# Window attention, forward and backward: attention products as 64x64 tiles only, and early gradient turns moved

## The chip, the cores and the metric

The kernel runs on one core of a Trainium2 chip. The metric is the device time of one execution, in microseconds. Before the change, 17 runs gave a median of 1991.69 us (1986.32 to 2002.65). TensorE (PE) multiplies, VectorE (DVE) and ScalarE (ACT) do the elementwise work and empty PSUM, GpSimd (POOL) and SyncE (SP) issue DMAs.

## The reference

An image `x` of 256 x 256 pixels with 384 channels is cut into 1024 windows of 8 x 8 pixels (64 tokens). In each window, self-attention with one head:

```python
qkv = xw @ wqkv
q, k, v = qkv[..., :C], qkv[..., C:2 * C], qkv[..., 2 * C:]
p = softmax(einsum('bqc,bkc->bqk', q, k) * C ** (-0.5), axis=-1)
o = einsum('bqk,bkc->bqc', p, v) @ wo
```

The outputs are `o` and, for a given `grad_out`, the gradients of `x` (`out_1`), `wqkv` (`out_2`) and `wo` (`out_3`). All data are bf16.

## The kernel before

The weights are merged first: `A` holds wq times the transpose of wk (with the scale), `B` holds wv times wo, and `AT_sb`, `BT_sb` their transposes. Per window, with tokens `x` and output gradient `d`, the kernel then needs `y` (from `x` and `A`) and `z` (from `d` and `BT`) to form the scores and the gradient of the probabilities; `uq` = x B and `vq` = x AT as values; and the products of the probabilities `P` and of their score gradients `dS` with `uq`, `vq`, `z`, `y`, `x` and `d`. The output `o` is P times `uq`. The gradient of `x` (the sums named `pd`) is the transpose of P times `z`, plus the transpose of dS times `y`, plus dS times `vq`. `Uq` (dS times x, named `pu` in PSUM) and `Wq` (the transpose of P times d, `pw`) feed the weight gradients.

Work goes in 128 quads. A quad is 4 tiles `t` of 128 partitions, and a tile is two windows: window 0 in partitions 0 to 63 (`LO`), window 1 in 64 to 127 (`HI`). The program is a software pipeline over quads, written out by hand: `step(c, b, a, ahead)` (L330) works on three quads at once. Each engine executes its instructions in the order in which the code issues them. In a step stand, in this order: the scores of quad `b` (`scores`, L179, 24 small products into `sd`); its softmax and softmax gradient in six pieces (`soft`, L191, on DVE and ACT) between the eight projections that make `uq` and `vq` (`uv`, L230); the projection of `a`'s gradient to `z` (`project` kind 0); a DMA transpose of `ps`, which holds P and dS side by side (`turn`, L240, giving `PS`, that is P and dS turned); the loads of the quad three ahead; a piece of the weight gradient (`filler(1)`: twelve products `pg`, added on DVE to `GF_acc`, L317); attention of `c` for tiles 0 and 1 (`attend`, L250); the projection of `a`'s tokens to `y` (`project` kind 1); `to_tokens` (L174), a DMA transpose of `yz`, which gives `z` and `y` with tokens in partitions, `tok`; another filler; and attention of `c` for tiles 2 and 3.

TensorE can be used as one array of 128 x 128, as two column halves (128*64 in the profile), or as four tiles of 64 x 64, which work side by side. In `attend`, `both` (L258) issues four products of 64 x 64 (row half in, row half out: LO to LO, LO to HI, HI to LO, HI to HI). "Straight" products write the half that they read; "crossed" ones write the other half, and their two sums then lie in two PSUM banks, one called outer. `po` and `pd` were crossed, `pu` and `pw` straight. `token_part` (L265) multiplies `ps` with `tok`, contracting over all 128 partitions, P with `z` in one half and dS with `y` in the other, as 128*64 products. Around it, the switch `split[0]` (L149) makes the projection to `y` and the filler between the pairs issue each product as two column halves.

PSUM has eight banks in one pool (`ring`); each sum takes a bank, and its next use waits until the last one is copied out. The DMA transposes of `tok`, `PS`, and of the loaded gradient and tokens (`load_turn`, L129: `dT` and `xT` of the quad two ahead) and the loads of `x` all stand in SP's queue, in the order of the code. POOL's queue holds the loads of the gradient and the stores of both outputs (L296 to L301). For the first quads, TensorE does the turns instead (`turn_on_pe`, L137): the gradients of quads 1 to 3 are turned inside the softmax of the step that projects them (`grad_turn`, L144 and L349). Behind the last step, `weight_gradients` (L380) finishes.

Of the kernel before, what the change touches and what calls it, by code (L numbers as in the profile page):

```python
# [22 lines left out]
def kernel(  # L23
# [124 lines left out]
    ALL = False  # L148
    split = [ALL]  # L149

    def product(out, lhsT, rhs, start, stop):
        if split[0]:
            for h in (LO, HI):
                nc.tensor.matmul(out[h], lhsT=lhsT[:, h], rhs=rhs, start=start, stop=stop)  # L154
        else:
            nc.tensor.matmul(out, lhsT=lhsT, rhs=rhs, start=start, stop=stop)  # L156

    ENG = {"D": nc.vector.tensor_copy, "A": nc.scalar.copy}

    def project(st, kind, mo):  # L160
        if kind == 0 and mo == 0:
            st["yz"] = qp.tile([P, CK, QUAD, 4, WT], BF16, tag="yz", name="yz")
        yz = st["yz"]
        wgt, src = ((BT_sb, st["dT"]), (A_sb, st["xT"]))[kind]
        pj = ring.tile([P, QUAD, 2, WT], F32, tag="r")
        for m in range(CK):
            product(pj[:].rearrange("p t w k -> p (t w k)"), wgt[:, m, mo * P:(mo + 1) * P], src[:, :, m, :],
                    m == 0, m == CK - 1)
        if kind == 0:
            ENG[EV["z"][mo]](out=yz[:, mo, :, 0:4:3, :], in_=pj[:])  # L170
        else:
            ENG[EV["y"][mo]](out=yz[:, mo, :, 1:3, :], in_=pj[:])  # L172

    def to_tokens(st):  # L174
        st["tok"] = tok = qp.tile([P, CK, QUAD, 2, P], BF16, tag="tok", name="tok", bufs=3)
        nc.sync.dma_start_transpose(out=tok[:].rearrange("p m t b k -> p (m t b) k"),
                                    in_=st["yz"][:].rearrange("p m t s k -> p (m t s k)"))

    def scores(st):  # L179
        yz, xT = st["yz"], st["xT"]  # L180
# [10 lines left out]
    def soft(st, step):  # L191
# [25 lines left out]
        elif step == 4:  # L217
            st["pr"] = pr = sm.tile([P, QUAD, WT], F32, tag="pr", name="pr")
            for w, h in ((0, LO), (1, HI)):
                nc.vector.tensor_tensor(out=pr[h, :, :], in0=sd[h, :, w, :], in1=st["Pb"][h, :, :], op=ALU.mult)  # L220
            st["D"] = D = sm.tile([P, QUAD], F32, tag="D", name="D")
            nc.vector.tensor_reduce(out=D[:], in_=pr[:], axis=AX.X, op=ALU.add)
        else:
            pd = sm.tile([P, QUAD, WT], F32, tag="pd")
            nc.vector.tensor_tensor(out=pd[:], in0=st["Pb"][:], in1=over_k(st["D"][:]), op=ALU.mult)
            ps = st["ps"]
            for w, h, o in ((0, LO, HI), (1, HI, LO)):
                nc.vector.tensor_tensor(out=ps[o, :, w, :], in0=st["pr"][h, :, :], in1=pd[h, :, :], op=ALU.subtract)

    def uv(st, t, part):  # L230
        if t == 0 and part == 0:
# [10 lines left out]
        nc.sync.dma_start_transpose(out=dst[:].rearrange("p t s k -> p t (s k)"),  # L242
                                    in_=st["ps"][:].rearrange("p t w k -> p (t w k)"))

    def turned(st, n, t, h):
        if n in ("PT", "ST"):
            return st["PS"][h, t, int((n == "ST") == (h == LO)), :]
        return st[n][h, t, :]

    def attend(st, pair):  # L250
# [4 lines left out]
        def bank(name):  # L255
            return ring.tile([P, C], F32, tag="r", name=name)

        def both(straight, crossed, t, outer, **flags):  # L258
            for h, o, (dst, lhs, rhs), fl in ((LO, LO, straight, {}), (LO, HI, crossed, flags), (HI, LO, crossed, flags),
                                              (HI, HI, straight, {})):  # L260
                at = dst if dst is not crossed[0] else dst[outer if h == LO else 1 - outer]
                nc.tensor.matmul(at[o, :], lhsT=turned(st, lhs, t, h), rhs=st[rhs][h, t, :],  # L262
                                 **{"start": True, "stop": True, **fl})

        def token_part(t, pd, outer, **flags):  # L265
            for w, o in ((0, HI), (1, LO)):
                nc.tensor.matmul(pd[outer if w == 0 else 1 - outer][o, :], lhsT=st["ps"][:, t, w, :],  # L267
                                 rhs=st["tok"][:, :, t, w, :], **flags)

        def keep(name, dst, src):  # L270
            for outer in (0, 1):
                sb = ob.tile([P, C], BF16, tag=name, name=name)
                nc.scalar.copy(out=sb[:], in_=src[outer][:])  # L273
                stores.append((dst, sb, outer))

        t0, t1 = pair
        stores = []
        pu = [bank("pu")]
        po = [bank("po") for outer in (0, 1)]
        pd = [bank("pd") for outer in (0, 1)]  # L280
        token_part(t0, pd, 1, start=True, stop=False)
        both((pu[0], "ST", "xq"), (po, "PT", "uq"), t0, 1)
        (nc.vector.tensor_copy if t0 else nc.scalar.copy)(out=st["Uq"][:, t0, :], in_=pu[0][:])
        pw = [bank("pw")]
        both((pw[0], "Pb", "dq"), (pd, "ST", "vq"), t0, 1, start=False, stop=True)
        nc.vector.tensor_copy(out=st["Wq"][:, t0, :], in_=pw[0][:])
        pu.append(bank("pu"))
        both((pu[1], "ST", "xq"), (po, "PT", "uq"), t1, 0)
        keep("o", out_0, po)
        nc.vector.tensor_copy(out=st["Uq"][:, t1, :], in_=pu[1][:])  # L290
        pw.append(bank("pw"))
        both((pw[1], "Pb", "dq"), (pd, "ST", "vq"), t1, 0, start=True, stop=False)
        nc.vector.tensor_copy(out=st["Wq"][:, t1, :], in_=pw[1][:])
        token_part(t1, pd, 0, start=False, stop=True)
        keep("d", out_1, pd)
        for dst, sb, outer in stores:  # L296
            if outer:
                nc.gpsimd.dma_start(out=windows(dst, st, 2 * t1 + 1, 1), in_=sb[LO, :])
                nc.gpsimd.dma_start(out=windows(dst, st, 2 * t0, 1), in_=sb[HI, :])
            else:  # L300
                nc.gpsimd.dma_start(out=windows(dst, st, 2 * t0 + 1), in_=sb[:])  # L301

    fill = []

# [25 lines left out]
    def step(c, b, a, ahead):  # L330
# [24 lines left out]
        if b is not None and c is None:  # L355
            turn_blocks(woT_sb, wo_sb)
# [12 lines left out]
        C_(attend, (2, 3))  # L369

    G_ON_PE, X_ON_PE = 4, 1
# [45 lines left out]
    with tc.manual_schedule(engines=MANUAL):  # L417
# [31 lines left out]
        split[0] = False  # L449
        filler(1 << 30)  # L450
        weight_gradients(last)

# [29 lines left out]
```

## Time and profile before

| | |
|---|---|
| median of 17 runs | 1991.69 us |
| the profiled execution | 1994.89 us |
| its span, first to last instruction | 1993.1 us |
| instructions | 52529 |
| granted TensorE clock, mean | 0.999 |
| DMA moved | 423.66 MB, mean 213 GB/s |
| SP's queue (q1): packets, share of 16 engines | 935984, 80.9% |
| POOL's queue (q0): packets, share of 16 engines | 98304, 31.1% |

A row of the profile's timeline gives start, length (both in us), engine, line of the code, operation, tiles out<-in, tile shape of a matmul, shape of the data and count; rows that follow each other with the same form are merged. Matmuls are pipelined, so the length of one includes its way through the array; the distance between starts tells the pace. A row of the groups gives the total busy time, the mean of one in ns, and the idle time ahead of it with who ended it.

### The profile page before, as it was taken

Reading aid. Unit: us, or ns where it says so; the run is one execution under the profiler, and the core shown is the slowest. Engines: PE = TensorE matmul, PEld = TensorE weight load, DVE = VectorE, ACT = ScalarE, POOL = GpSimd, SP = SyncE. Lnnn points to the kernel's source line nnn. Section 1 sums busy time; section 2 is a strip of 40 time slices with the busy share of each in tenths; the row PEclk is TensorE's granted clock in tenths of the full one; section 3 lists DMA queues with packets and bytes.
Section 4 is the critical chain, followed back from the end, with each engine's and each line's share of the span. In section 5 each row is a group of like instructions: output and inputs, shape, how many; then the busy total and the mean of one; then the engine's idle time right before and its main releaser. Section 6 shows DMA issues by size and latency. Waiting matters only on the chain. (4 is left out here: it accounts for less than half of the span.)

```text
span 1993.1 us, 52529 instructions
## 1 busy us (share of the span) xinstructions
PE 1967.3 (99%) x19487; PEld 1123.5 (56%) x19487; DVE 1259.6 (63%) x2860; ACT 1461.7 (73%) x3357; POOL 1122.5 (56%) x2054
## 2 busy tenths in 40 slices
PE   8999999999999999999999999999999999999999
PEld 4555555555555555555555555555555555555555
DVE  4666666666666656666666666666666666666666
ACT  6877777777777777777777777777777777777774
POOL 2655555555556555555555565556555555555553
PEclk9999999999999999999999999999999999999999
DMA  7999999999999999999999999999999999999994
GB/s 168 215 218 215 203 226 213 218 207 229 213 217 225 213 207 222 220 215 212 215 222 215 222 210 220 216 222 224 219 219 216 210 221 207 217 223 213 219 210 107
DMA packets 1036032, 423.66 MB, mean 213 GB/s; under 512 B 918016, under 2 KB 1011200, under 8 KB 1035776
## 3 DMA queue, kind: packets, MB, share of 16 engines
q1 hardware_dynamic: 935984, 267.85, 80.9%
q0 software_dynamic: 98304, 151.39, 31.1%
q8 instruction: 152, 2.49, 0.5%
q10 hardware_dynamic: 1488, 1.08, 0.2%
q14 instruction: 104, 0.85, 0.2%
HBM read 101.84 MB, written 101.84 MB: 102 GB/s over the span
## 5 line engine op out<-in xcount | busy, mean ns | idle before, releaser
L301 POOL DMA_DIRECT2D out_dram<-o x256 | 139.1, 543 | 679.7 <-ACT o L273 666.1
L317 DVE TENSOR_TENSOR GF_acc<-pg,GF_acc 128x384 f32<-128x384 f32 x258 | 143.9, 558 | 526.1 <-PE pg L154 372.2
L273 ACT CAST o<-po 128x384 bf16<-128x384 f32 x512 | 221.7, 487 | 247.8 <-issue 247.6
L156 PEld LDWEIGHTS <-xT 128*128 128x128 bf16 x3072 | 291.7, 98 | 183.2 <-issue 1.5
L156 PE MATMUL pj<-AT_sb,xT 128*128 128x384 bf16 x1536 | 333.5, 326 | 0.8 <-DVE dT L91 0.8
L156 PE MATMUL pj<-B_sb,xT 128*128 128x384 bf16 x1536 | 333.5, 326 | 0.0
L127 POOL DMA_DIRECT2D dq<-in_grad_out_dram x512 | 273.9, 546 | 77.0 <-DMA out_dram<-o 35.6
L156 PE MATMUL pj<-dT,BT_sb 128*128 128x512 bf16 x1152 | 271.3, 381 | 14.4 <-DMA dT<-dq 6.6
L154 PE MATMUL pj<-xT,A_sb 128*64 128x512 bf16 x2304 | 270.2, 379 | 0.0
L238 ACT CAST uq<-pj 128x384 bf16<-128x384 f32 x512 | 247.5, 483 | 30.1 <-PE pj L156 26.0
L238 ACT CAST vq<-pj 128x384 bf16<-128x384 f32 x512 | 250.1, 488 | 2.4
L273 ACT CAST d<-pd 128x384 bf16<-128x384 f32 x512 | 227.4, 512 | 0.2 <-ACT o L273 0.2
L156 PEld LDWEIGHTS <-xq 128*128 128x128 bf16 x1572 | 153.5, 98 | 114.8 <-issue 0.3
L154 PEld LDWEIGHTS <-xq 128*64 128x64 bf16 x3000 | 166.5, 110 | 90.3
L216 ACT COPY ps<-Pb 64x256 bf16<-64x256 bf16 x256 | 103.2, 403 | 149.6 <-DVE Pb L213 148.1
L170 ACT CAST yz<-pj 128x512 bf16<-128x512 f32 x384 | 207.0, 642 | 3.2 <-PE pj L156 2.0
L172 ACT CAST yz<-pj 128x512 bf16<-128x512 f32 x384 | 208.4, 658 | 0.8 <-PE pj L154 0.6
L156 PEld LDWEIGHTS <-BT_sb 128*128 128x128 bf16 x1152 | 111.8, 98 | 141.4 <-DMA dT<-dq 14.7
L154 PEld LDWEIGHTS <-A_sb 128*64 128x64 bf16 x2304 | 130.8, 110 | 97.7 <-issue 0.4
L156 PE MATMUL pg<-Uq,xq 128*128 128x384 bf16 x1032 | 181.6, 326 | 0.0
L267 PE MATMUL pd<-tok,ps 128*64 128x384 bf16 x1024 | 177.5, 344 | 0.0
L262 PE MATMUL pu<-xq,PS 64*64 64x384 bf16 x1024 | 175.0, 335 | 2.4 <-DMA PS<-ps 2.2
(87 smaller groups left out, 3386.5 us busy)
## 6 DMA issues: line engine op xcount, KB each, us to landing
xq<-in_x_dram SPq DMA_DIRECT2D x512, 96.0 KB, 4.1
dq<-in_grad_out_dram POOLq DMA_DIRECT2D x512, 96.0 KB, 3.9
out_dram<-o POOLq DMA_DIRECT2D x256, 96.0 KB, 4.3
out_dram<-o POOLq DMA_DIRECT2D x512, 48.0 KB, 4.4
out_dram<-d POOLq DMA_DIRECT2D x256, 96.0 KB, 4.5
out_dram<-d POOLq DMA_DIRECT2D x512, 48.0 KB, 4.5
tok<-yz SPq DMA_TRANSPOSE x128, 8.3
PS<-ps SPq DMA_TRANSPOSE x128, 4.9
```

Of the source, the lines that this page charges most:

```text
L127: nc.gpsimd.dma_start(out=dq[:, t, :], in_=windows(grad_out, st, 2 * t))
L154: nc.tensor.matmul(out[h], lhsT=lhsT[:, h], rhs=rhs, start=start, stop=stop)
L156: nc.tensor.matmul(out, lhsT=lhsT, rhs=rhs, start=start, stop=stop)
L170: ENG[EV["z"][mo]](out=yz[:, mo, :, 0:4:3, :], in_=pj[:])
L172: ENG[EV["y"][mo]](out=yz[:, mo, :, 1:3, :], in_=pj[:])
L216: nc.scalar.copy(out=ps[h, :, w, :], in_=Pb[h, :, :])
L238: cp(out=dst[:, t, :], in_=pj[:])
L262: nc.tensor.matmul(at[o, :], lhsT=turned(st, lhs, t, h), rhs=st[rhs][h, t, :], **{"start": True, "stop": True, **fl})
L267: nc.tensor.matmul(pd[outer if w == 0 else 1 - outer][o, :], lhsT=st["ps"][:, t, w, :], rhs=st["tok"][:, :, t, w, :], **flags)
L273: nc.scalar.copy(out=sb[:], in_=src[outer][:])
L301: nc.gpsimd.dma_start(out=windows(dst, st, 2 * t0 + 1), in_=sb[:])
L317: nc.vector.tensor_tensor(out=GF_acc[:, f, ma, :], in0=pw[:], in1=GF_acc[:, f, ma, :], op=ALU.add)
```

## The change

There are two parts.

*The attention products.* `attend` now issues six rounds per pair of tiles, each of four 64 x 64 products (`slot`). `po` becomes straight, one bank per tile. The token part is no longer 128*64: P times `z` and dS times `y` are 64 x 64 products, crossed, and each half of the two `pd` banks collects three of them. For that, dS is also kept unturned (`dS`, one more DVE subtraction in `soft` 5), and `tok` holds `z` and `y` of a window in the same partitions. So `gather` copies `z` and `y` on DVE out of `yz` into `zy`, which `to_tokens` transposes. `yz` has one buffer instead of two. The copy of the first `pw` of each pair goes to ACT; the other `pw` and the `pu` go to DVE. The stores of `o` are two whole ones per pair instead of one whole and two halves; those of `d` stay. The split is gone: the projection to `y` and all fillers are 128 x 128 products.

*The early turns.* The gradient of quads 1 to 3 is turned on TensorE behind the last pair of the step ahead of the one that projects it, and the blocks of `wo` are turned after step 1 instead of inside step 0.

```diff
-    def grad_turn(st):
-        if 0 < st["i"] < G_ON_PE:
-            turn_on_pe(st, "dq", "dT")
...
     def product(out, lhsT, rhs, start, stop):
-        if split[0]:
-            for h in (LO, HI):
-                nc.tensor.matmul(out[h], lhsT=lhsT[:, h], rhs=rhs, start=start, stop=stop)
-        else:
-            nc.tensor.matmul(out, lhsT=lhsT, rhs=rhs, start=start, stop=stop)
+        nc.tensor.matmul(out, lhsT=lhsT, rhs=rhs, start=start, stop=stop)
...
+    def gather(st, kind):
+        if kind == 0:
+            st["zy"] = qp.tile([P, 2, CK, QUAD, 2, WT], BF16, tag="zy", name="zy")
+        src = st["yz"][:, :, :, 0:4:3, :] if kind == 0 else st["yz"][:, :, :, 1:3, :]
+        nc.vector.tensor_copy(out=st["zy"][:, kind, :, :, :, :], in_=src)
+
     def to_tokens(st):
-        st["tok"] = tok = qp.tile([P, CK, QUAD, 2, P], BF16, tag="tok", name="tok", bufs=3)
-        nc.sync.dma_start_transpose(out=tok[:].rearrange("p m t b k -> p (m t b) k"),
-                                    in_=st["yz"][:].rearrange("p m t s k -> p (m t s k)"))
+        st["tok"] = tok = qp.tile([P, 2, CK, QUAD, P], BF16, tag="tok", name="tok", bufs=3)
+        nc.sync.dma_start_transpose(out=tok[:].rearrange("p b m t k -> p (b m t) k"),
+                                    in_=st["zy"][:].rearrange("p b m t s k -> p (b m t s k)"))
...
+            st["dS"] = dS = qp.tile([P, QUAD, WT], BF16, tag="dS", name="dS")
+            nc.vector.tensor_tensor(out=dS[:], in0=st["pr"][:], in1=pd[:], op=ALU.subtract)
...
+        def slot(straight, crossed, start=False, stop=False):
+            for h in (LO, HI):
+                dst, lhs, rhs, t = straight
+                products = [(h, dst[h, :], lhs, rhs, t, {"start": True, "stop": True})]
+                lhs, rhs, t = crossed
+                o = OTHER[h.start]
+                dst = pd[int((t == t0) == (h == LO))]
+                products.append((o, dst[o, :], lhs, rhs, t, {"start": start, "stop": stop}))
+                for o, dst, lhs, rhs, t, flags in products if h == LO else products[::-1]:
+                    nc.tensor.matmul(dst, lhsT=operand(st, lhs, t, h), rhs=operand(st, rhs, t, h), **flags)
...
+        slot((pw[t0], "Pb", "dq", t0), ("Pb", "z", t0), start=True)
+        nc.scalar.copy(out=st["Wq"][:, t0, :], in_=pw[t0][:])
+        slot((pw[t1], "Pb", "dq", t1), ("dS", "y", t0))
+        nc.vector.tensor_copy(out=st["Wq"][:, t1, :], in_=pw[t1][:])
+        slot((pu[t0], "ST", "xq", t0), ("Pb", "z", t1), start=True)
+        nc.vector.tensor_copy(out=st["Uq"][:, t0, :], in_=pu[t0][:])
+        slot((po[t0], "PT", "uq", t0), ("dS", "y", t1))
+        o0 = keep("o", po[t0])
+        slot((pu[t1], "ST", "xq", t1), ("ST", "vq", t0), stop=True)
+        nc.vector.tensor_copy(out=st["Uq"][:, t1, :], in_=pu[t1][:])
+        slot((po[t1], "PT", "uq", t1), ("ST", "vq", t1), stop=True)
...
-        A(grad_turn)
...
         C_(attend, (0, 1))
-        split[0] = True
+        A(gather, 0)
         for mo in range(CK):
             A(project, 1, mo)
+        A(gather, 1)
         A(to_tokens)
         filler(1)
-        split[0] = ALL
         C_(attend, (2, 3))
...
             step(get(i - 1), get(i), get(i + 1), get(i + AHEAD) if i >= 0 else None)
+            if 0 < i + 2 < G_ON_PE:
+                turn_on_pe(sts[i + 2], "dq", "dT")
+            if i == 1:
+                turn_blocks(woT_sb, wo_sb)
```

On TensorE, where `attend (2, 3)` begins behind the filler (`pg`), the rows before were these; the numbers tell tiles of one name apart.

```order
L154 MATMUL pg_18039<-Wq_17396,xq_16231 64x384
L267 LDWEIGHTS ps_17606
L267 MATMUL pd_18069<-tok_17467,ps_17606 64x384
L267 LDWEIGHTS ps_17606
L267 MATMUL pd_18068<-tok_17467,ps_17606 64x384
L262 LDWEIGHTS PS_17654
L262 MATMUL pu_18065<-xq_16801,PS_17654 64x384
L262 LDWEIGHTS PS_17654
L262 MATMUL po_18067<-uq_17573,PS_17654 64x384
L262 LDWEIGHTS PS_17654
L262 MATMUL po_18066<-uq_17573,PS_17654 64x384
```

Now the pair begins like this (here the first pair of a step):

```order
L266 MATMUL pw_17110<-dq_15985,Pb_16755 64x384
L266 LDWEIGHTS Pb_16755
L266 MATMUL pd_17114<-tok_16627,Pb_16755 64x384
L266 LDWEIGHTS Pb_16755
L266 MATMUL pd_17113<-tok_16627,Pb_16755 64x384
L266 LDWEIGHTS Pb_16755
L266 MATMUL pw_17110<-dq_15985,Pb_16755 64x384
L266 LDWEIGHTS Pb_16755
L266 MATMUL pw_17111<-dq_15985,Pb_16755 64x384
L266 LDWEIGHTS dS_16805
L266 MATMUL pd_17114<-tok_16627,dS_16805 64x384
```

The products with `tok` were the pair's own first and last rounds; now they are the crossed products of its first four rounds, and the products with `PS` come from the third round on.

On DVE, the rows from the first filler's sum to the maxima of the next scores were:

```order
L317 TENSOR_TENSOR GF_acc<-pg,GF_acc 128x384
L286 CAST Wq<-pw 128x384
L290 CAST Uq<-pu 128x384
L293 CAST Wq<-pw 128x384
L317 TENSOR_TENSOR GF_acc<-pg,GF_acc 128x384
L283 CAST Uq<-pu 128x384
L286 CAST Wq<-pw 128x384
L290 CAST Uq<-pu 128x384
L293 CAST Wq<-pw 128x384
L196 TENSOR_REDUCE mx<-sd 64x4 x2
```

and are now:

```order
L225 TENSOR_TENSOR dS<-pr,pd 128x256
L313 TENSOR_TENSOR GF_acc<-pg,GF_acc 128x384
L283 CAST Wq<-pw 128x384
L285 CAST Uq<-pu 128x384
L289 CAST Uq<-pu 128x384
L167 COPY zy<-yz 128x1536 x2
L313 TENSOR_TENSOR GF_acc<-pg,GF_acc 128x384
L283 CAST Wq<-pw 128x384
L285 CAST Uq<-pu 128x384
L289 CAST Uq<-pu 128x384
L191 TENSOR_REDUCE mx<-sd 64x4 x2
```

The two gathers stand between the first pair's last cast and the second filler's sum.

At the start, the 12 turning products of quad 1 moved in TensorE's order from inside the softmax of step 0 to just ahead of its scores, and those of quads 2 and 3 from steps 1 and 2 to the ends of steps 0 and 1.

More of the change, by code (lines that the diff above doesn't have):

```diff
@@ L256, in bank @@
             return ring.tile([P, C], F32, tag="r", name=name)
[L258 to L274, printed above, removed]
+        def slot(straight, crossed, start=False, stop=False):
[8 more added lines that the diff above has]
+                    nc.tensor.matmul(dst, lhsT=operand(st, lhs, t, h), rhs=operand(st, rhs, t, h), **flags)
@@ L276, in attend, with keep @@
+        def keep(name, src):
+            sb = ob.tile([P, C], BF16, tag=name, name=name)
+            nc.scalar.copy(out=sb[:], in_=src[:])
+            return sb
         t0, t1 = pair
-        stores = []
-        pu = [bank("pu")]
-        po = [bank("po") for outer in (0, 1)]
+        pw = {t: bank("pw") for t in pair}
+        pu = {t0: bank("pu")}
         pd = [bank("pd") for outer in (0, 1)]
-        token_part(t0, pd, 1, start=True, stop=False)
-        both((pu[0], "ST", "xq"), (po, "PT", "uq"), t0, 1)
@@ L283, in attend @@
[L283 to L301, printed above, removed]
+        po = {t0: bank("po")}
@@ new lines, in attend @@
+        o0 = keep("o", po[t0])
+        slot((pu[t1], "ST", "xq", t1), ("ST", "vq", t0), stop=True)
+        nc.vector.tensor_copy(out=st["Uq"][:, t1, :], in_=pu[t1][:])
+        slot((po[t1], "PT", "uq", t1), ("ST", "vq", t1), stop=True)
+        o1 = keep("o", po[t1])
+        d = [keep("d", pd[outer]) for outer in (0, 1)]
+        nc.gpsimd.dma_start(out=windows(out_0, st, 2 * t0), in_=o0[:])
+        nc.gpsimd.dma_start(out=windows(out_0, st, 2 * t1), in_=o1[:])
+        nc.gpsimd.dma_start(out=windows(out_1, st, 2 * t0 + 1), in_=d[0][:])
@@ L303 @@
+        nc.gpsimd.dma_start(out=windows(out_1, st, 2 * t1 + 1, 1), in_=d[1][LO, :])
+        nc.gpsimd.dma_start(out=windows(out_1, st, 2 * t0, 1), in_=d[1][HI, :])
     fill = []
@@ L448 @@
                 held = []
-        split[0] = False
         filler(1 << 30)
```

12 lines of the change are left out of this document (6 added, 6 removed).

## The prediction

> **What bounds the kernel now.** I read the page's busy times first, then TensorE's timeline through one whole step in the middle of the run, then who TensorE waits for, and last the queue that feeds it.
>
> The first fence is the head of the page.
>
> ```profile
> span 1993.1 us, 52529 instructions
> PE 1967.3 (99%) x19487; PEld 1123.5 (56%) x19487; DVE 1259.6 (63%) x2860; ACT 1461.7 (73%) x3357; POOL 1122.5 (56%) x2054
> ```
>
> TensorE is busy 99% of the span, and the next engine, ACT, has a quarter of its time free. So I look for what TensorE spends on something else than streaming columns. The next fence is its timeline (start, length, engine, line, out<-in, tile shape) from the filler that stands ahead of `attend (0, 1)` to the scores that follow `attend (2, 3)`.
>
> ```profile
> 1000.29 2.11 PE L156 MATMUL pg<-Uq,xq 128*128 128x384 bf16 x12
> 1002.33 0.35 PE L267 MATMUL pd<-tok,ps 128*64 128x384 bf16 x2
> 1002.62 0.35 PE L262 MATMUL pu<-xq,PS 64*64 64x384 bf16 x1
> ...
> 1002.63 0.35 PE L262 MATMUL pu<-xq,PS 64*64 64x384 bf16 x1
> 1002.80 0.32 PE L262 MATMUL pw<-dq,Pb 64*64 64x384 bf16 x1
> ...
> 1002.97 0.32 PE L262 MATMUL pu<-xq,PS 64*64 64x384 bf16 x1
> ...
> 1003.13 0.32 PE L262 MATMUL pw<-dq,Pb 64*64 64x384 bf16 x1
> ...
> 1003.39 0.35 PE L267 MATMUL pd<-tok,ps 128*64 128x384 bf16 x2
> 1003.58 2.11 PE L154 MATMUL pj<-xT,A_sb 128*64 128x512 bf16 x18
> 1005.52 2.12 PE L154 MATMUL pg<-Uq,xq 128*64 128x384 bf16 x24
> 1007.47 0.33 PE L267 MATMUL pd<-tok,ps 128*64 128x384 bf16 x2
> ...
> 1008.87 0.87 PE L156 MATMUL sd<-xT,yz 128*128 128x64 bf16 x24
> ...
> 1015.42 1.79 PE L156 MATMUL pg<-Uq,xq 128*128 128x384 bf16 x10
> ```
>
> Lengths overlap, so only starts count. A step is 15.13 us, from filler to filler (1000.29 to 1015.42). The 24 half-width filler products take 1005.52 to 1007.47, 1.95 us, and nothing changes shape behind them. That is 12 rounds of 0.16 us, and a round of four 64*64 tiles that follows another such round also starts 0.16 us later (1002.97 to 1003.13). A change of shape costs more: the full filler takes 2.04 us (1000.29 to 1002.33), 0.09 more than 1.95, because 128*64 products follow it. From 128*64 to 64*64 stand 0.29 us (1002.33 to 1002.62), and from the last 64*64 round to 128*64 stand 0.26 (1003.13 to 1003.39). The first round in the new shape is followed after 0.18 (1002.62 to 1002.80). So the two pairs cost 1.25 us (1002.33 to 1003.58) and 1.40 us (1007.47 to 1008.87), where twelve rounds of 0.16 would be 1.92.
>
> The waits of TensorE come next: first in the first 110 us, then in the rest (total, times, longest).
>
> ```profile
> PE pj L156 <- ACT dT L89: 4.8, 3, 1.6
> ```
>
> ```profile
> PE pj L156 <- DMA dT<-dq: 6.6, 8, 1.6
> ```
>
> In the steady part TensorE waits 6.6 us, in eight places, for the turned gradients `dT` that come through SP's queue; nothing else there is larger. That queue is the second thing to watch: here is SP's issue of transposes in the same stretch, with the DVE row that finishes `ps`.
>
> ```profile
> 1000.50 4.56 SPq L176 DMA_TRANSPOSE tok<-yz  x1
> ...
> 1011.34 1.20 SPq L242 DMA_TRANSPOSE PS<-ps  x1
> ...
> 1015.23 4.66 SPq L176 DMA_TRANSPOSE tok<-yz  x1
> ```
>
> ```profile
> 1000.48 0.85 DVE L228 TENSOR_TENSOR ps<-pr,pd 64x256 bf16<-64x256 f32 x2
> ```
>
> `ps` is complete at 1001.33, yet its transpose is issued at 1011.34: SP runs 10 us behind its data. It issues one thing after another, and from `tok` to `tok` is 14.73 us. So SP's round is shorter than TensorE's step of 15.13, but only by 0.4 us, and the few waits for `dT` are the times when it fell too far behind.
>
> **The change, part by part.** All sums are made against the profiled execution, 1994.9 us (span 1993.1 and 1.8 around it). The median of the runs shown is 1991.7, so 3.2 us are taken off at the end.
>
> *The attention products as 64*64 tiles.* Each pair had four rounds of 64*64 and two of 128*64; it now has six of 64*64. The columns streamed are the same, twelve rounds per step. What goes is shape changes: before, a step changed into 128*64, into 64*64, back to 128*64 (first pair), into 64*64, back, and into 128*128 for the scores: six. The change also takes the split from the second projection and filler, so both pairs now stand between 128*128 products: four changes. Each pair is then 0.09 (entry, as before `tok`), 0.19 for the first round (0.18 and the rounding), four rounds of 0.16, and 0.26 to 0.29 on the way out: 1.18 to 1.21. Before, they were 1.25 with 0.09 ahead of it and 1.40, together 2.74. Two pairs now come to 2.36 to 2.42, so 0.32 to 0.38 per step; I take 0.34. No row shows 128*128 straight to 64*64 or back; the bounds are 0.09 (into 128*64) and 0.13 (0.29 less 0.16, into 64*64) in, 0.10 to 0.13 out, so an entry at the high end takes 0.08 per step back. Over 128 steps 0.34 is 44 us; with the dear entry it is 33.
>
> *The split taken from the projection and filler.* 18 half-width products take 1.94 us (1003.58 to 1005.52) and 24 half-width fillers 1.95. Nine full ones and twelve full ones stream the same columns; the full filler's 2.04 less the 0.09 is 1.95 as well. Nothing either way, apart from the shape changes counted above.
>
> *Gathering `z` and `y`.* Two DVE copies of 128x1536 bf16 per step are new, and one subtraction (`dS`); one DVE cast of `pw` or `pu` per step goes to ACT. These rows price it, together with the casts of `y` on ACT and the DVE row that follows the second filler.
>
> ```profile
> L211 DVE RECIPROCAL ri<-rs 128x4 f32<-128x4 f32 x128 | 22.8, 178 | 4.4
> ...
> L290 DVE CAST Uq<-pu 128x384 bf16<-128x384 f32 x256 | 140.2, 548 | 0.0
> ...
> L319 DVE CAST GFb<-GF_acc 128x384 bf16<-128x384 f32 x6 | 2.2, 360 | 0.2
> ```
>
> ```profile
> 1004.88 1.62 ACT L172 CAST yz<-pj 128x512 bf16<-128x512 f32 x3
> ```
>
> ```profile
> 1007.68 0.56 DVE L317 TENSOR_TENSOR GF_acc<-pg,GF_acc 128x384 f32<-128x384 f32 x1 [3.01 <-PE pg L154]
> ```
>
> No row shows a bf16 copy from SBUF to SBUF. A four-element operation takes 0.178 us, so the cast out of SBUF spends 0.182 on 384 elements and the cast out of PSUM 0.370. For 1536 elements that gives 0.178 + 4 x 0.182 = 0.91 us and 0.178 + 4 x 0.370 = 1.66 us. I take 0.91, since the copy is nearest to the SBUF row. DVE was idle for 3.01 us ahead of that `GF_acc`, so the first gather is free. The second must wait for `y`'s last cast, 4.17 us after the pair's start (1006.50 less 1002.33). Ahead of it in DVE's queue is nothing late, but behind it stand the filler's `GF_acc` and the casts of the second pair. The last round of `attend (2, 3)` uses the bank that `GF_acc` frees. From the first pair's start that round is due at 1.10 (the pair) + 1.94 + 1.95 + 0.09 + 0.19 + 0.64 = 5.91 us. With 0.91 the gather ends at 5.08, `GF_acc` can begin about when its filler ends, and 0.56 later, at some 5.7, the bank is free. So the gather costs nothing, with 0.2 us to spare. At 1.66 it would cost: that is a rival below. The page "VectorE: DVE Perf Modes" of the Trainium skill, under "What auto-detection actually checks", says a one-source 16-bit copy inside SBUF runs at four elements a cycle; from its table I estimate 0.56 us, by which the spare time would be 0.5 us and the sum the same. No run here shows it yet.
>
> SP's `to_tokens` now waits for the gather instead of the cast, some 1 us later; behind it in SP's queue stand the next step's `dT` and `xT`, whose reader is TensorE. It costs nothing as long as SP is 10 us behind its data anyway; if SP caught up, this 1 us would come off its slack. `yz` has one buffer instead of two: its next writer is ACT's cast of the next `z`, and its last readers, the scores and the second gather, stand a whole softmax ahead of that; free.
>
> *Stores.* Per pair there are five instead of six, with the same bytes; these rows give time to landing.
>
> ```profile
> out_dram<-o POOLq DMA_DIRECT2D x256, 96.0 KB, 4.3
> out_dram<-o POOLq DMA_DIRECT2D x512, 48.0 KB, 4.4
> ```
>
> Half the bytes land no sooner, so two halves made one whole can only relieve the DMA engines and so SP's transposes. I put this at nothing to 0.3 us per SP round, unpriced by any row, and use it only as a reason why SP may keep up.
>
> *The early turned gradients.* They were turned inside the softmax of steps 0 to 2, right ahead of the projection that reads them, and TensorE waited 4.8 us for the copies. Behind the step ahead, the copies have the scores and eight projections as cover, 24 products of 0.16 or 3.8 us against copies of some 0.5 us each. The 12 transposes themselves remain. One projection also ran slow after such a wait:
>
> ```profile
> 28.41 3.73 PE L156 MATMUL pj<-dT,BT_sb 128*128 128x512 bf16 x9 [1.58 <-ACT dT L89]
> ```
>
> It should take 2.1 us, as the 18 half-width ones do. So the gain is 4.8 to 6.4 us; I take 6. The copies now stand ahead of the step's first maxima in DVE's queue, about 0.7 us in three steps, with the whole softmax to hide in.
>
> *The sum.* 1994.9 - 44 - 6 = 1944.9. TensorE's step falls to some 14.8 us, equal to SP's round of 14.73. So I let the waits for `dT` grow from 6.6 us to some 15, plus 8: 1952.9, and against the median 1949.7. I say 1950.
>
> **The rivals.** *SP's queue takes half of it back.* For it: SP is 10 us behind and never idle, and TensorE already waits for `dT`. Against: the stores become fewer, and SP's round was 14.73 where nothing held it. If its mean round cannot go below about 14.97 us, 0.17 x 128 = 22 us are gained, plus 6: 1991.7 - 28 = 1964, anywhere from 1958 to 1982. Chance 0.22.
>
> *SP's queue sets the whole pace already.* Then TensorE only waits more: 0 to 6 us gained, 1986 to 1992. The waits would have to be the rule, and they are eight in 128 steps. Chance 0.08, half of it within 0.2% (4 us, about what a measurement of this kernel can tell from no change).
>
> *Weights do not come early enough in long runs of 64*64 rounds.* Then every round takes the 0.18 or 0.19 us of the first: four rounds by 0.03 by two pairs, 0.24 back, 0.10 left, 13 us: 1991.7 - 13 - 6 = 1973. The rows show 0.16 for the third and fourth rounds. Chance 0.08.
>
> *The gather is slow and the second pair waits for its last bank.* The price: at 1.66 us the second gather ends at 4.17 + 1.66 = 5.83, `GF_acc` at 6.39, 0.48 after the round is due, with the semaphore some 0.53. Less 0.34 that is 0.19 per step, 24 us slower; with the 6 of the start, 1991.7 + 18 = 2010. Waiting begins when the gather takes over 1.1 us, and the sum turns at about 1.5. For it: no row shows such a copy. Against: the SBUF row. Chance 0.09.
>
> *Two row halves cannot write one bank together.* `po` was crossed, its two row halves in two banks; now it is straight, both in one. If those then ran one behind the other, each of two rounds in each pair would take 0.16 more, 0.64 per step: 0.30 slower, 38 us, and 1991.7 + 38 - 6 = 2024. Against it: `pu` is already straight, and its halves start at 1002.62 and 1002.63 with the next round 0.18 later. Chance 0.03. The page "TensorEngine Tiling (Array Packing)" of the Trainium skill, under "Restrictions and Gotchas", says that different row tiles cannot access the same bank at once; by that rule it would be so, and the trace does not agree.
>
> **How the numbers follow.** My forecast has 0.50: 1950, from 1935 (no more waits, the small exit, the clock gain) to 1960 (the dear entry). The rivals have 0.22, 0.08, 0.08, 0.09 and 0.03. Faster by over 0.2%: 0.50 + 0.22 + 0.08 + 0.04 = 0.84; within 0.2%: 0.04; slower: 0.12. The range from 1935 to 1982 leaves out the slower cases and the case without gain, 0.20.
>
> **What would show it.** In the changed kernel's timeline: six rounds per pair, the first two 0.19 apart and the others 0.16; 1.2 us from the end of the filler to what follows; a step of about 14.8 us; no `pj <- ACT dT` waits in the first 60 us. The gather row near 0.9 us or below. If the step is 14.8 where nothing waits but `pj <- DMA dT` has grown to tens of us, SP was the limit; if `po <- DVE GF_acc` appears in each step, the gather was. If pairs still take 1.35 us, the prices of the shape changes are wrong, and with them the main term.

## The result, and the profile after

The changed kernel has a median of 1944.80 us (8 runs, 1940.36 to 1949.50), beside 1990.66 for the kernel before (47 runs). The ratio is 0.9769, with a 95% interval from 0.9754 to 0.9783: 2.3% faster, 46 us. The profiled execution took 1949.5 us, with a span of 1947.5.

The head of the page after:

```profile
span 1947.5 us, 48767 instructions
PE 1927.2 (99%) x17859; PEld 1076.3 (55%) x17859; DVE 1380.1 (71%) x3116; ACT 1535.4 (79%) x3485; POOL 1006.9 (52%) x1798
```

TensorE still fills 99% of the span. DVE and ACT do more than before (1259.6 and 1461.7 us there), and both have a fifth or more of their time left. So the gain has to show in TensorE's own pace. Its timeline, again from the filler ahead of `attend (0, 1)`, with one row for each round of the first pair:

```profile
986.70 2.11 PE L145 MATMUL pg<-Uq,xq 128*128 128x384 bf16 x12
988.74 0.35 PE L266 MATMUL pw<-dq,Pb 64*64 64x384 bf16 x1
...
988.93 0.33 PE L266 MATMUL pd<-tok,dS 64*64 64x384 bf16 x2
...
989.09 0.32 PE L266 MATMUL pu<-xq,PS 64*64 64x384 bf16 x1
...
989.25 0.32 PE L266 MATMUL po<-uq,PS 64*64 64x384 bf16 x1
...
989.26 0.32 PE L266 MATMUL po<-uq,PS 64*64 64x384 bf16 x1
989.42 0.32 PE L266 MATMUL pu<-xq,PS 64*64 64x384 bf16 x1
...
989.58 0.32 PE L266 MATMUL po<-uq,PS 64*64 64x384 bf16 x1
...
989.84 2.12 PE L145 MATMUL pj<-xT,A_sb 128*128 128x512 bf16 x9
991.80 2.11 PE L145 MATMUL pg<-Wq,xq 128*128 128x384 bf16 x12
993.84 0.35 PE L266 MATMUL pw<-dq,Pb 64*64 64x384 bf16 x1
...
994.94 0.87 PE L145 MATMUL sd<-xT,yz 128*128 128x64 bf16 x24
...
1001.50 1.30 PE L145 MATMUL pg<-Wq,xq 128*128 128x384 bf16 x7
```

The step is 14.80 us (986.70 to 1001.50), where it was 15.13. A pair takes 1.10 us from its first round to what follows (988.74 to 989.84, and 993.84 to 994.94), with 0.09 ahead of it: 2.38 for both, where it was 2.74. Inside a pair the second round starts 0.19 after the first, and the others follow after 0.16 to 0.17. The two row halves of `po`, which now write one bank, start at 989.25 and 989.26, and the next round follows 0.16 later.

TensorE's waits over the whole span:

```profile
PE pu L266 <- DMA PS<-ps: 5.6, 5, 2.3
PE pj L145 <- DMA dT<-dq: 4.4, 4, 1.7
...
PE pg L145 <- DVE GF_acc L313: 0.5, 1, 0.5
```

Before, beside the 6.6 us for `dT`, TensorE also waited for `PS`:

```profile
PE pu L262 <- DMA PS<-ps: 2.2, 2, 1.6
```

The 4.8 us of `pj <- ACT dT` are gone. The two turned tiles that come through SP's queue, `dT` and `PS`, cost 10 us together, where they cost 8.8 before. DVE's gather costs nothing that shows: the one wait of 0.5 us for `GF_acc` stands at 1915.6, behind the last step. The gather itself, in DVE's groups and in its timeline of this step:

```profile
L167 DVE COPY zy<-yz 128x1536 bf16<-128x1536 bf16 x256 | 147.2, 575 | 194.7 <-ACT yz L161 192.2 <-ACT yz L159 2.5
```

```profile
986.89 0.85 DVE L223 TENSOR_TENSOR ps<-pr,pd 64x256 bf16<-64x256 f32 x2
...
992.77 0.56 DVE L167 COPY zy<-yz 128x1536 bf16<-128x1536 bf16 x1 [1.45 <-ACT yz L161]
993.95 0.56 DVE L313 TENSOR_TENSOR GF_acc<-pg,GF_acc 128x384 f32<-128x384 f32 x1 [0.62 <-PE pg L145]
```

The copy takes 0.575 us. The second one ends at 993.33, and DVE then idles 0.62 us until the filler ends. Last, SP's queue in the same step, and the stores' rows of the page:

```profile
986.41 4.36 SPq L171 DMA_TRANSPOSE tok<-zy  x1
...
996.37 1.23 SPq L239 DMA_TRANSPOSE PS<-ps  x1
...
1000.95 4.44 SPq L171 DMA_TRANSPOSE tok<-zy  x1
```

```profile
out_dram<-o POOLq DMA_DIRECT2D x512, 96.0 KB, 4.1
...
tok<-zy SPq DMA_TRANSPOSE x128, 7.7
PS<-ps SPq DMA_TRANSPOSE x128, 5.2
```

`ps` is complete at 987.74 and its transpose issued at 996.37: SP is 8.6 us behind its data, about as far as before (10 in the step shown; over all steps the median is 8.6 now and was 9.0). This round of SP takes 14.54 us, and its mean over the run is 14.85, worked out from the `tok` issues, where it was 15.21. SP has sped up together with TensorE.

Where the 45.6 us between the two spans came from: the median step, worked out from the starts of the scores, went from 15.13 to 14.80, 128 x 0.33 = 42 us; the start up to the scores of the fifth step went from 76.8 to 72.4 us, 4.4; what single steps take above the median, from the fifth on, was 14.2 us in all and is 14.6.

### The profile page after: what moved, and what is told of

Read it like the earlier page. It is cut to its first block, busy times and chain, and to the rows that moved or that the text cites. A ratio compares the mean times of both kernels' runs of the same rounds, so it can differ in the third digit from the quotient of the medians.

```text
span 1947.5 us, 48767 instructions
## 1 busy us (share of the span) xinstructions
PE 1927.2 (99%) x17859; PEld 1076.3 (55%) x17859; DVE 1380.1 (71%) x3116; ACT 1535.4 (79%) x3485; POOL 1006.9 (52%) x1798
## 4 chain that ended last, share of the span: by engine, by line
PE 82%; DMA 6%; issue 5%; POOL 3%; ACT 3%; DVE 1%; ACTq 0%; POOLq 0%
PE pj L145 43%; PE pg L145 22%; PE pw L266 5%; PE sd L145 4%; PE pu L266 4%; PE po L266 3%; DMA PS<-ps 2%; DMA dT<-dq 2%; POOL dq L127 1%; DMA dq<-in_grad_out_dram 1%; DMA out_dram<-o 1%; ACT uq L235 1%; POOL out_dram L297 1%; POOL out_dram L293 1%; POOL out_dram L294 0%
## 5 line engine op out<-in xcount | busy, mean ns | idle before, releaser
L145 PEld LDWEIGHTS <-xq 128*128 128x128 bf16 x3072 | 300.3, 98 | 226.2 <-issue 2.2
L281 ACT CAST Wq<-pw 128x384 bf16<-128x384 f32 x256 | 123.3, 482 | 211.0 <-PE pw L266 195.9
L167 DVE COPY zy<-yz 128x1536 bf16<-128x1536 bf16 x256 | 147.2, 575 | 194.7 <-ACT yz L161 192.2
L145 PE MATMUL pj<-xT,A_sb 128*128 128x512 bf16 x1152 | 272.4, 382 | 0.0
L145 PE MATMUL pg<-Uq,xq 128*128 128x384 bf16 x1536 | 270.6, 326 | 0.5 <-DVE GF_acc L313 0.5
L145 PE MATMUL pg<-Wq,xq 128*128 128x384 bf16 x1536 | 270.4, 326 | 0.0
L297 POOL DMA_DIRECT2D out_dram<-d x256 | 178.6, 697 | 10.3 <-issue 7.2
```

The lines of the kernel that those rows point to most:

```text
L167: nc.vector.tensor_copy(out=st["zy"][:, kind, :, :, :, :], in_=src)
L281: nc.scalar.copy(out=st["Wq"][:, t0, :], in_=pw[t0][:])
L297: nc.gpsimd.dma_start(out=windows(out_1, st, 2 * t0, 1), in_=d[1][HI, :])
```

## The experiments

The theory after the result: TensorE sets the pace, two shape changes fewer per step save a third of a microsecond, and the moved turns save some 5 us. The rivals: the split or the gather matter by themselves; and SP's queue, not TensorE, decides what of such a saving arrives.

**The early turns alone (e1).** The kernel before, with only the turns moved:

```diff
-        A(grad_turn)
...
-        if b is not None and c is None:
-            turn_blocks(woT_sb, wo_sb)
...
+            if 0 < i + 2 < G_ON_PE:
+                turn_on_pe(sts[i + 2], "dq", "dT")
+            if i == 1:
+                turn_blocks(woT_sb, wo_sb)
```

> The kernel before, with the early turns alone moved behind the last pair of the step ahead. My theory (each part gives its own time, the start about 6 us of the 46): 1990.7 - 6 = 1985, between 1983 and 1987, with the waits for the turned gradient gone from the first 60 us. Rival (SP's queue sets the whole pace, so time gained at the start is waited away later): 1990 to 1991, with longer waits for dT.

Measured: 1986.14 us beside 1990.76, ratio 0.9967 (0.9948 to 0.9987): 4.6 us less, and the waits for ACT's `dT` are gone.

**The tiles alone (e2).** The changed kernel with the turns put back:

```diff
+        if a is not None and 0 < a["i"] < G_ON_PE:
+            turn_on_pe(a, "dq", "dT")
...
+        if b is not None and c is None:
+            turn_blocks(woT_sb, wo_sb)
...
-            if 0 < i + 2 < G_ON_PE:
-                turn_on_pe(sts[i + 2], "dq", "dT")
-            if i == 1:
-                turn_blocks(woT_sb, wo_sb)
```

> The kernel after, with the early turns put back inside the softmax. My theory: the start's 6 us come back, 1944.8 + 6 = 1951, between 1949 and 1953, and the step stays 14.80 us. Rival (the two parts are not independent, because SP's queue catches up in a slower start): 1945 to 1948.

Measured: 1952.17, ratio 0.9803 (0.978 to 0.9826), 7.4 us more than with them. Its waits show what came back:

```profile
PE pj L145 <- ACT dT L89: 4.8, 3, 1.6
```

So by the medians the turns are worth 4.6 us in one kernel and 7.4 in the other, and the tiles some 39 to 41. The 7.4 is the less certain number: it rests on four runs, its interval overlaps that of the changed kernel, and in the two profiles the scores of the fifth step start at 74.6 and 72.4 us, 2.2 apart.

**The split (e3, e4).** Once taken out of the kernel before, once put back into the changed one:

```diff
-        split[0] = True
```

> The kernel before, with the split alone taken out: the projection to y and the filler between the pairs are 128*128, attention as it was. My theory (changes of array shape are what costs): the first pair now leaves from 128*64 to 128*128 and the second enters again, 0.10 + 0.09 us per step more, 128 times: +24, 2015, between 2010 and 2019. Rival (half-width products are dear by themselves, and the change gains because they are gone): faster than 1990.

Measured: 2005.03, ratio 1.0072 (1.005 to 1.0094), 14 us slower: the way that was expected, but less than the 24. The columns streamed are the same, but a pair of `token_part` is now entered from 128*128 and left to 128*128. TensorE's timeline:

```profile
1006.95 0.35 PE L267 MATMUL pd<-tok,ps 128*64 128x384 bf16 x2
1007.23 2.12 PE L156 MATMUL pj<-xT,A_sb 128*128 128x512 bf16 x9
```

From the last 128*64 round to the projection stand 0.28 us instead of 0.16 to 0.19. The step grew from 15.13 to 15.28, 0.15 us for two more changes, 19 us in all; SP had more time then, and the excess over the median step fell from 14.2 to 7.5 us, which leaves 12 of the 14 measured. The 0.19 per step that was expected was thus too high by 0.04, and the rest of the miss is SP's.

```diff
...
+        split[0] = True
         for mo in range(CK):
             A(project, 1, mo)
...
         filler(1)
+        split[0] = False
...
```

> The kernel after, with the split put back on the projection to y and the filler between the pairs. My theory: the pairs still stand between products of another shape, two changes per pair, and columns are the same: 1944.8 within 3 us. Rival (half-width products are dear): slower by 10 us or more; and if a change between 64*64 and 128*64 were cheaper than one between 64*64 and 128*128, faster by 5 us or more.

Measured: 1947.40, ratio 0.9777 (0.9755 to 0.9799), beside 0.9769 for the changed kernel: no difference. Where pairs of 64*64 tiles stand on both sides, it is the same whether the products between them are full or half as wide. The split is worth something only next to other 128*64 products.

**The price of a change of shape (e5, e6).** In each pair, a small product is put between the third and the fourth round, whose sum a later round overwrites: 64 columns as one 128*128 product, or the same columns as two 64*64 ones, which change no shape.

```diff
+        nc.tensor.matmul(pu[t1][:, 0:WT], lhsT=ident[:], rhs=st["xq"][:, t0, 0:WT], start=True, stop=True)
```

> The kernel after, with one more 128*128 product of 64 columns between the third and the fourth round of each pair, into a bank that the fifth round overwrites: two more changes of shape per pair. It adds work that the outputs do not use. My theory: out 0.10, in 0.09, first round 0.025 slower, and some 0.03 to 0.06 for the product: 0.25 to 0.28 us per pair, 256 pairs: +64 to +72 us, 2009 to 2017. Rival (a change of shape costs nothing by itself, the old pairs waited for something else): +8 to +16 us, 1953 to 1961.

```diff
+        for h in (LO, HI):
+            nc.tensor.matmul(pu[t1][h, 0:WT], lhsT=ident[h, h], rhs=st["xq"][h, t0, 0:WT], start=True, stop=True)
```

> The control of the run before: the same place, but two 64*64 products of 64 columns, so no change of shape. It adds work that the outputs do not use. My theory: 0.03 to 0.1 us per pair, +8 to +26 us, 1953 to 1971; the difference from the run before is the price of two changes, 0.2 us or 51 us in 256 pairs. Rival: within 10 us of the run before.

Measured: 2000.29 (ratio 1.0046, 1.0027 to 1.0066) for the full product and 1950.87 (0.9796, 0.9771 to 0.982) for the tiles, 49.4 us apart, 0.193 us for each of the 256 pairs. Both times lie below what was expected for them (2009 to 2017, 1953 to 1971). The steps tell why: the median is 15.31 us with the full product and 14.86 with the tiles, so two changes take 0.23 us, and the excess over the median step, 14.6 us in the changed kernel, is 0 and 6.8 here. The slower step gave SP time, which hides a part of the price in the whole. TensorE's timeline of the first and of the second:

```profile
1004.37 0.32 PE L266 MATMUL pu<-xq,PS 64*64 64x384 bf16 x1
1004.63 0.20 PE L286 MATMUL pu<-xq,ident 128*128 128x64 bf16 x1
1004.77 0.35 PE L266 MATMUL po<-uq,PS 64*64 64x384 bf16 x1
...
1004.95 0.32 PE L266 MATMUL pu<-xq,PS 64*64 64x384 bf16 x1
```

```profile
1007.81 0.32 PE L266 MATMUL pu<-xq,PS 64*64 64x384 bf16 x1
...
1007.97 0.19 PE L287 MATMUL pu<-xq,ident 64*64 64x64 bf16 x1
...
1008.13 0.33 PE L266 MATMUL pd<-vq,PS 64*64 64x384 bf16 x2
```

Out of the tiles is 0.26 (1004.37 to 1004.63), 0.10 more than a round; from the 64 columns back into tiles 0.14, and the first round there takes 0.18. The small tiles themselves start on the pace of 0.16. This prices a change between 64*64 and 128*128 by itself: 0.11 us. Whether the array's change or the loading of weights around it takes that time, these runs do not tell.

So two changes fewer are not the whole of the 0.33. Twelve rounds at the pace inside a pair take 1.95 us. The two pairs with their six changes took 2.74 before, 0.13 us for each change, and take 2.38 with four, 0.11 for each. The changes that are left are also the cheaper ones: out of 128*64 into 64*64 stood 0.29 us, 0.13 more than a round.

**The gather four times as long (e7).**

```diff
-        A(gather, 1)
+        for again in range(4):
+            A(gather, 1)
```

> The kernel after, with the second gather issued four times instead of once (the same copy again), so that it holds DVE 1.72 us longer. My theory (the last round of the second pair waits for the bank that GF_acc frees, with some 0.8 us to spare now, since a copy took 0.575): GF_acc ends some 1.7 us later, 0.95 us past the round's due time: 128 x 0.95 = +121, 2066, between 2050 and 2085, with waits of po for GF_acc in each step. Rival (DVE has time for it, the filler's sum is not awaited): 1945 to 1950.

Measured: 2023.93, ratio 1.0165 (1.014 to 1.0189), 79 us more than the changed kernel. DVE's timeline and TensorE's waits:

```profile
1003.34 2.35 DVE L167 COPY zy<-yz 128x1536 bf16<-128x1536 bf16 x4 [1.46 <-ACT yz L161]
1005.60 0.55 DVE L313 TENSOR_TENSOR GF_acc<-pg,GF_acc 128x384 f32<-128x384 f32 x1
```

```profile
PE sd L145 <- DVE GF_acc L313: 61.1, 123, 0.5
```

The mechanism is the one expected: copies hold up `GF_acc`, and TensorE waits for the bank. The price put on it was too high: it is the next scores that wait for the bank, not the last round of `attend (2, 3)`. The next scores can begin once the `GF_acc` shown ends at 1006.15, and they start at 1006.21. The step grew to 15.47, by 0.67, for 1.8 us more of copying (2.35 less 0.56), so the gather has 1.1 us to spare.

**One `o` store in two halves, as before (e8).**

```diff
-        nc.gpsimd.dma_start(out=windows(out_0, st, 2 * t0), in_=o0[:])
+        nc.gpsimd.dma_start(out=windows(out_0, st, 2 * t0, 1), in_=o0[LO, :])
+        nc.gpsimd.dma_start(out=windows(out_0, st, 2 * t0 + 1, 1), in_=o0[HI, :])
```

> The kernel after, with one of the two stores of o per pair cut in halves again, six stores per pair as before. Theory A (the stores relieved the DMA engines, and that is why SP kept up with the shorter step): waits of TensorE for dT and PS grow by 10 us or more, 1955 or above. Theory B (SP follows TensorE's step whatever the stores): within 3 us of 1944.8.

Measured: 1962.37, ratio 0.9852 (0.9828 to 0.9877), 17.6 us more than with five stores. The bytes are the same, and the step in which nothing waits is still 14.80. The waits:

```profile
PE pj L145 <- DMA dT<-dq: 15.7, 15, 2.9
PE pu L266 <- DMA PS<-ps: 3.8, 6, 1.2
```

The waits for `dT` have grown from 4.4 to 15.7 us, those for `PS` fell from 5.6 to 3.8, and what single steps take above the median went from 14.6 to 27.0. These 12.4 us are all of the 11.6 by which the two profiled executions differ (spans of 1959.1 and 1947.5); the profiled run of the changed kernel was the longest of its eight. SP's mean round went from 14.85 to 14.95, again some 12 us in 128 steps. So between 12 and 18 of the 46 us, 17.6 by the medians, rest on a line that does not touch TensorE.

**No filler (e9, e10).** To see the pace that SP's queue keeps by itself, TensorE's steps are made some 4 us shorter: the weight-gradient products in the loop go, and with them DVE's sums, so two outputs lack most of what they should add up.

```diff
-        filler(1)
         C_(attend, (0, 1))
...
-        filler(1)
         C_(attend, (2, 3))
...
-        filler(1 << 30)
```

> The kernel after without the fillers: the partial sums of the weight gradients are left out except those of the last group, so two outputs are not the reference's. TensorE's step falls by 24 products of 0.16, from 14.80 to 10.9 us. This shows what SP's queue can do when TensorE does not set the pace. If SP's round has a floor of about 14.5 us (its mean of 14.8 was its own), the time is 128 x 14.5 + 40 = 1900; if it merely follows TensorE, the time falls to ACT's 12.0 us of work per step or to SP's bare issue, 1540 to 1700.

Measured: 1962.01 (2 runs), ratio 0.9858 (0.9827 to 0.9888): 17 us slower than the changed kernel, with less work. TensorE is busy for 1614 us instead of 1927 and waits:

```profile
PE pu L266 <- DMA PS<-ps: 205.7, 95, 6.2
PE pj L145 <- DMA dT<-dq: 102.6, 53, 3.9
```

This is not a case that the expectation had: it gave 1900, or 1540 to 1700. SP's timeline of one round, with the DVE row that finished the `ps` which is turned in it:

```profile
1001.63 4.63 SPq L171 DMA_TRANSPOSE tok<-zy  x1
...
1013.28 1.21 SPq L239 DMA_TRANSPOSE PS<-ps  x1
...
1017.15 4.45 SPq L171 DMA_TRANSPOSE tok<-zy  x1
```

```profile
1000.12 0.85 DVE L223 TENSOR_TENSOR ps<-pr,pd 64x256 bf16<-64x256 f32 x2
```

`ps` is complete at 1000.97 and issued at 1013.28, 12.3 us later; the median over the run is 11.8, where it is 8.6 in the changed kernel. So SP does not wait for the other engines here, they wait for SP, and its mean round is 15.04. That SP's rows fill its time says nothing: they fill 94% of it in this run, and 94% in e5 too, where TensorE's step of 15.31 sets the pace. So the queue, with the transfers behind it, takes about 15 us also when TensorE could go faster. This is not a fixed floor, since the changed kernel's round is 14.85; but it shows no slack under that. The single round of 14.73 before, on which the prediction built, was no proof of slack: the mean was 15.21. Whether SP's issuing or the DMA engines set these 15 us stays open: the engines moved 216 GB/s in this run, 217 in the changed kernel and 213 before, and in all three they are 90% busy or more in nearly every slice of the page.

The same with one `o` store in halves (the edits of e8 and e9 together):

> The same without fillers, and with one store of o per pair in halves. If the DMA engines bound the run without fillers and halves load them more, it is slower than the run without fillers by 10 us or more (0.1 us per step or more); if halves cost the DMA engines nothing, the same within 5 us.

Measured: 1963.77 (2 runs), ratio 0.9866 (0.9836 to 0.9897), no difference from e9 that can be told. With TensorE out of the way, a sixth store cost 1.8 us by the medians of two runs each, and SP's mean round stayed the same (15.05 and 15.04); with TensorE at work it cost 17.6. The count of stores is thus not all of it; when they fall on the transposes may matter too. These runs do not settle it.

**Other orders of the queues (e11, e12).** If SP's queue is what TensorE waits for, its order might help: e11 turns the gradient of the quad three ahead, ahead of `to_tokens`, and `PS` ahead of `xT`.

```diff
+        if late_x is not None:
+            turn_in(late_x, "xq", "xT")
...
         A(gather, 1)
+        if early_d is not None:
+            turn_in(early_d, "dq", "dT")
         A(to_tokens)
```

> The kernel after with another order in SP's queue: dT of the quad three ahead is turned ahead of to_tokens instead of in the next step, and PS goes ahead of xT. My theory (what is left above 14.80 us per step are waits for PS and dT in SP's queue, some 10 to 15 us in all): these waits go, 1944.8 - 10 = 1935, between 1930 and 1940. Rival (the waits come from single slow transfers, whatever the order, or move to xT and tok): 1943 to 1947.

Measured: 1943.63 (6 runs, 1937.27 to 1956.14), ratio 0.9766 (0.9737 to 0.9795), the same, as the rival had it. The waits go to another transpose (in the profiled run, the longest of the six):

```profile
PE pj L150 <- DMA xT<-xq: 17.2, 11, 2.7
```

And e12 takes the loads of `x` from SP's queue to POOL's.

```diff
-            nc.sync.dma_start(out=xq[:, t, :], in_=windows(x, st, 2 * t))
+            nc.gpsimd.dma_start(out=xq[:, t, :], in_=windows(x, st, 2 * t))
```

> The kernel after with the loads of x issued from POOL's queue instead of SP's; bytes and order of the data are the same. The run without fillers showed that the queues need about 15 us per step by themselves. Theory A (it is SP's issuing, one thing after another, that needs them): SP's round loses four issues, it catches up with its data, the waits for PS and dT go, 1944.8 - 10 = 1935 or below. Theory B (it is the DMA engines, whoever issues): SP stays some 8 us or more behind its data, 1942 to 1950, or slower if POOL's later stores and loads hold ACT up.

Measured: 2026.31 to 2061.89 over six runs, ratio 1.0261 (1.0216 to 1.0305). The four shortest have a median of 2034.2, 89 us above the changed kernel. TensorE's waits, SP's largest wait for a load, and two rows of the page, all from the shortest run:

```profile
PE pu L266 <- DMA PS<-ps: 49.6, 39, 4.8
PE pj L145 <- DMA dT<-dq: 17.0, 15, 1.9
```

```profile
SPq L134 <- DMA dq<-in_grad_out_dram: 153.0, 69, 6.4
```

```profile
out_dram<-o POOLq DMA_DIRECT2D x512, 96.0 KB, 6.1
...
tok<-zy SPq DMA_TRANSPOSE x128, 11.6
```

The median step is still 14.80 us. What single steps take above it went from 14.6 to 91.2 us, and these 76.6 us are all of the 76.9 by which the two spans differ (2024.4 and 1947.5). TensorE's two waits make up 56.6 of them, being 66.6 us where they were 10. SP issues less, but it now waits for the loads of the gradient, which stand in POOL's queue between those of `x` and behind the stores: in the changed kernel a gradient had landed 16.5 us before its transpose was issued (median), and here the transpose is issued 0.2 us behind the landing. What stands behind it in SP's queue, `xT`, `PS` and `tok`, waits with it. The transfers also take longer: each `tok` lands after 11.6 us instead of 7.7, and the stores after 6.1 instead of 4.1. So this run does not decide between the two theories: it took the issues from SP, but it made POOL's queue too slow for its loads.

No version here beats the changed kernel by more than can be measured.

## Why the prediction was right

*The bound and the main term.* Right in mechanism and size. 0.34 us per step was taken, 0.33 came: 42 us of the 46. The pairs now take 2.38 us, inside the 2.36 to 2.42 worked out, and the dear entry did not come: into 64*64 it is 0.09, out 0.10, as in the cheap rows. e5 against e6 shows that a change of shape costs by itself (0.11 us, against the 0.09 to 0.13 that the prediction read from its rows), e3 that the split had been there to avoid two of them, e4 that nothing else hung on the split.

*The start.* 6 taken, 4.6 and 7.4 measured (e1, e2), and 4.4 between the two profiles.

*The gather.* Priced at 0.91 us from the SBUF row, measured 0.575, below the lower bound: the four-element operation and the cast did not foretell a plain copy of bf16. The estimate of 0.56 us from the table on the page "VectorE: DVE Perf Modes" of the Trainium skill, under "Side-by-side: where the cycles go for N=2048 bf16", agrees with the trace's 0.575. Nothing hung on that, since it was covered either way. The 0.5 us of spare time worked out from it were too much by the prediction's own sum: `GF_acc` cannot begin before its filler ends, at about 5.0, however short the gather is. The room was put at 0.2 us; e7 shows 1.1, because the bank goes to the scores. The rival needed a gather of over 1.1 us to wait at all; by e7 it is about 1.7 (0.575 and 1.1).

*The waits for SP.* From 6.6 to 15 us for `dT`, the sum said. They fell to 4.4, and `PS` rose from 2.2 to 5.6, which was not foreseen. In sum 8.8 became 10.0, so nearly all of the 8 us laid aside were unused. The main term and the start brought some 2 us less each than was taken, and the median before is 1 us lower in the longer series; together this makes the 5 us between 1950 and 1944.8.

*The stores.* This is the term that was sized wrong: "nothing to 0.3 us per SP round, unpriced by any row", left out of the sum. e8 puts it at 17.6 us. With six stores the change would have come to 1962, outside the forecast's own 1935 to 1960 and where the first rival stood (1964). So that rival had its facts nearly right: it named a mean round of 14.97 us as SP's limit, and SP's mean round is 14.95 in e8 and 15.04 in e9. What kept it from happening is that the change does without the sixth store. The argument against it, that SP's round "was 14.73 where nothing held it", was the weak one; a single round does not show the mean that a queue can hold. The other argument, that the stores become fewer, held, but it was in no sum. To that extent the forecast of 1950 was met by luck.

*The other rivals.* Rounds in long runs follow each other after 0.16 to 0.17, so the weights come early enough. The two row halves of `po` in one bank run together: they start at 989.25 and 989.26, and the next round 0.16 later. By the page "TensorEngine Tiling (Array Packing)" of the Trainium skill, under "Restrictions and Gotchas", different row tiles cannot access the same bank at once; the trace differs.

## What to carry to other kernels

On an engine that is busy 99% of the time, count the changes of tile shape, not only the columns: here each cost about 0.1 us (0.08 between 128*64 and 128*128 in e3, 0.11 between 64*64 and 128*128 in e5). Price one by the step in which nothing waits, since a slower step gives the queue behind it time and hides a part of the price. Before a saving on the bounding engine is put into a sum, find the pace of the engine or queue behind it with a run that leaves work of the first one out; a queue that keeps up may have nothing to spare. And look at the small edits around the main one: here one store less per pair let some 17 us of the saving through.

## What was not expected of the hardware

- Less work on TensorE made the kernel slower: 1962 us without the fillers, 1945 with them, at a granted clock of 0.941 instead of 0.999. The waits were for DMA transposes, so the lower clock need not be the cause; that was not tried. A projection that followed a wait of 3.27 us took 3.64 us there, where one without a wait takes 2.11.
- Two 48 KB stores in place of one of 96 KB cost 17.6 us over 256 pairs beside a busy TensorE, and nothing that can be told where TensorE waits for SP (e8, e10). Why is open.
- Loads moved to the other queue slowed the transposes left behind, from 7.7 to 11.6 us for `tok`, and made the loads that were already there late (e12).
